# Seven-product feed-forward units: prefix sums in PSUM instead of partial sums in SBUF

## The chip, the cores and the metric

The kernel runs on one core of a Trainium2 chip. The metric is device time in microseconds (us) of one execution. The core has TensorE (matrix products into PSUM, the accumulator memory of eight banks), VectorE, ScalarE, GpSimd (POOL) and 16 DMA engines. All transfers are issued by SyncE (SP), which takes its instructions strictly in order: a transfer that has to wait for a buffer holds up every transfer behind it.

## The reference

Two layers, each of a gated long convolution (A) and a feed-forward block (B), over 2048 tokens of width 1024, all in 32-bit floats:

```python
x = A_q
x = x + _A_ref(_layernorm(x), A_k, A_v, A_shift_k, A_ssm_k, A_ssm_D)
x = x + _B_ref(_layernorm(x), B_w1, B_b1, B_w2, B_b2)
x = x + _A_ref(_layernorm(x), A_k, A_v, A_shift_k, A_ssm_k, A_ssm_D)
x = x + _B_ref(_layernorm(x), B_w1, B_b1, B_w2, B_b2)
...
def _B_ref(x, w1, b1, w2, b2):
    h = jnp.einsum("bsd,df->bsf", x, w1) + b1
    r = jnp.where(h > zero, h, zero)
    out = jnp.einsum("bsf,fd->bsd", r * r, w2) + b2
```

The hidden width of the feed-forward block is 3584. The change touches the second product (`w2`) alone.

## The kernel before

The tokens are cut into four blocks of 512 (`T`), and each block of each layer is a unit: eight units, in the order `ORDER`. A unit does the feed-forward block for its 512 tokens: the first product (`m1` steps), the squared ReLU, the second product (`m2` or `w2` steps), and the sum with the residual. The convolution for later blocks runs beside the first five units on VectorE, POOL, ScalarE and a little TensorE.

Every float32 product is made of three products of rounded parts (`mm3`, lines 335 to 338): a matrix is split into a high and a low part, and high x high, high x low and low x high are added in PSUM. A weight tile (128 x 512) is loaded into a ring of eight raw tiles (`wr`), cast by ScalarE into its high part (line 1013), and VectorE subtracts to make the low part (line 1021). High and low lie together in a `whl` tile, of which there are six. Some split weights are written back to DRAM (`wd_...`, lines 1025 to 1029) and later loaded as a pair of 512 KB, without a split (line 1011). Raw tiles are loaded 8 steps ahead, pairs asked for 4 steps ahead, once the `whl` slot is free.

The order is written out by hand: the list `steps` holds one step per weight tile, and each pass of the main loop issues one step to TensorE, with the loads and splits for later steps. Work that has to come later is put into `Later` queues with a number of ticks; one tick is one step. `lag.at(3, f)` issues `f` three steps on.

Units 5, 6 and 7 (`WINO`) make the second product with seven block products in place of eight (Winograd's form of Strassen's scheme). The 512 tokens are two halves, the hidden dimension goes in 14 pairs of tiles, the 1024 columns are two halves. Products 0 and 1 use plain parts of the activations and of `w2`, product 2 a sum of activations with plain `w2`, product 3 plain activations with a combined weight, and 4, 5 and 6 sums of activations with combined weights. Activations are combined on the fly (`relu_w`); combined weights are made once, in units 4 and 5 (`make_t`), and kept in DRAM (`td`). A unit has four chunks of 3, 3, 4 and 4 pairs (`WCH`): the first product for the chunk's tiles, and then the seven products in the order `WORD` (the last chunk: `WORD_END`), each over the chunk's pairs, for two tiles of 128 tokens, into two PSUM banks. Four banks (`p2`) serve products alternately.

After each product `evict_w` takes the two banks into SBUF: added by VectorE to a partial sum of that product, or, in chunk 0 for products 0, 4, 5 and 6, copied by ScalarE. Products 1, 2 and 3 and a tile `x` start from the residual plus the bias; products 0, 4, 5 and 6 have partial sums of their own (`fx`, `fg`, `acc`). In the last chunk the table `WEND` says after which product which partial sums are merged (`merge_w`, VectorE adds in SBUF) and when each quadrant (token half x column half) is stored. The residual is loaded at tick 11 (`load_wacc`), the bias `b2` at tick 34 into one of two `px` buffers, and POOL adds it at tick 38 (`add_b2w`). The same `px` buffers take the next unit's rows, loaded from step 28 of the unit on by `prep_a` for its statistics, and during the last 90 steps by `prep_w`, which normalises and transposes them.

In the last chunk of units 6 and 7, product 0 takes one stored pair and products 1, 4 and 5 take four each; the other weight tiles are raw. In unit 5, products 4 and 5 of the last chunk are split for the first time there and stored.

Of the kernel before, what the change touches and what calls it, by code (L numbers as in the profile page):

```python
# [10 lines left out]
F32 = mybir.dt.float32  # L11
# [8 lines left out]
P = 128  # L20
T = 512
NT = T // P
# [29 lines left out]
WINO = (5, 6, 7)  # L52
# [2 lines left out]
T_KEPT, T_RATE, T_FIRST, T_AT = 10, 0.6, 10, (0, 3, 1, 2)  # L55
WCH = (3, 3, 4, 4)
WHALF = T // 2
WORD, WORD_END = (0, 1, 3, 4, 5, 6, 2), (0, 3, 5, 6, 4, 2, 1)
WEND = {0: (), 3: (), 5: ((1, 1, 5, 0),), 6: ((1, 1, 6, 5), (2, 1, 3, 6), (2, 0, 3), (3, 1, 6, "x"), (3, 1, 1, 0)),
        4: ((1, 1, 6, 4), (1, 0, 6), (2, 1, 5, 4), (2, 1, 2, 5)), 2: ((1, 0, 2),), 1: ((1, 0, 1),)}  # L60
AHEAD_F = (6, 5)
KEEP_F = 3
KEEP_M = 4
# [177 lines left out]
def tile_h3_mlp(ctx: ExitStack, tc: tile.TileContext, q, kT, vT, shk, ssmT, ssmD, w1, b1, w2, b2,  # L241
                fwd_t, pro_t, inv_t, sgn_t, out):
    nc = tc.nc
    V, A, G, PE, SY = nc.vector, nc.scalar, nc.gpsimd, nc.tensor, nc.sync
# [65 lines left out]
    def ps2():  # L310
        return ps.tile([P, 512], F32, name="p2", bufs=4)
# [20 lines left out]
        for o in tiles:  # L332
            held[slot.pop(id(o))[0]] = False

    def mm3(o, lh, ll, rh, rl, start, stop):
        PE.matmul(o, lh, rh, start=start, stop=False)  # L336
        PE.matmul(o, lh, rl, start=False, stop=False)  # L337
        PE.matmul(o, ll, rh, start=False, stop=stop)  # L338

    def hold(n):  # L340
        got = take(n)
# [542 lines left out]
    def add_wino(u):  # L884
        p0 = 0
        for c, n in enumerate(WCH):
            pairs = range(p0, p0 + n)
            p0 += n
            for f in range(2 * pairs[0], 2 * pairs[-1] + 2):
                for kh in range(2):  # L890
                    add("m1", u, f // FC, f % FC, kh)
            for j in WORD_END if c == len(WCH) - 1 else WORD:
                for p in pairs:
                    f = 2 * p + (j > 0)
                    wsrc.append(("m2", f // FC, int(j == 2), f % FC) if j < 3 else ("t", p, (j - 4) % 4, 0))
# [593 lines left out]
    lag = slag  # L1489
# [94 lines left out]
            rp[p] = [(q["hi"], q["lo"]), (h(st["hi"], 0), h(lo, 0)), (st["zh"][:, 3], st["zl"][:, 3]),  # L1584
                     (h(st["hi"], 1), h(lo, 1)), *((st["zh"][:, i], st["zl"][:, i]) for i in range(3))]

    def load_wacc(wacc, b):
        for j, (t0, h) in {1: (0, 0), 2: (0, 1), 3: (2, 0), 0: (0, 0)}.items():
            a = ml.tile([P, 2, 512], F32, name="acc", bufs=NT)
            if j:  # L1590
                SY.dma_start(a, X1[b][:, t0:t0 + 2, h * 512:(h + 1) * 512])
            wacc[j] = [a[:, n] for n in range(2)]
        for j, mk in ((4, mkfx), (5, mkfx), (6, mkfg), ("x", mkfk)):
            wacc[j] = [mk([P, T]) for _ in range(2)]
        for n in range(2):
            SY.dma_start(wacc["x"][n], X1[b][:, 2 + n, 512:])

    def add_b2w(st, wacc):
        for j, h in ((1, 0), (2, 1), (3, 0), ("x", 1)):
            for a in wacc[j]:  # L1600
                G.tensor_add(a, a, st["t"][:, h * 512:(h + 1) * 512])  # L1601

    def evict_w(os, wacc, j, c):
        for n in range(2):
            if c == 0 and j in (0, 4, 5, 6):
                A.copy(wacc[j][n], os[n])
            else:
                V.tensor_add(wacc[j][n], os[n], wacc[j][n])

    def merge_w(wacc, dx):  # L1610
        d, x = dx
        for n in range(2):
            V.tensor_add(wacc[d][n], wacc[d][n], wacc[x][n])

    def store_w(wacc, l, b, j):
        t0, h = {1: (0, 0), 2: (0, 1), 3: (2, 0), 6: (2, 1)}[j]
        for n in range(2):
            dst = tokens(out, b, t0 + n) if l else X2[b][:, t0 + n]
            SY.dma_start(dst[:, h * 512:(h + 1) * 512], wacc[j][n])

    def evict(os, accs, dh):
        d = slice(dh * 512, (dh + 1) * 512)
# [145 lines left out]
    owed = town = 0.0  # L1768
    fowed = 0.0
    accs = []  # L1770
    pa = None
    nxt = None
    cur_u = -1
# [7 lines left out]
    for s, (k, u, c, a, i, tts, w) in enumerate(steps):  # L1781
        if s < 2 * AHEAD_0:
            continue
        l, b = ORDER[u]
        if u != cur_u:
            cur_u = u
            if u:
                xT = nxt
            bst = {}
            if u in WINO:  # L1790
                wacc, rp = {}, {}
                lag.at(11, load_wacc, wacc, b)
                lag.at(34, load_b2, bst)
                lag.at(38, add_b2w, bst, wacc)
            else:
                if not (u and direct[u - 1]):
                    accs = []
                    lag.at(5, load_acc, accs, b)
                lag.at(12, load_b2, bst)
                lag.at(16, add_b2, bst, accs)  # L1800
        soon.tick()
        phase[0] = "" if len(tts) == NT else "x" if k == "m1" else "b" if tts[0] else ""
        if phase[0] == "x":
# [7 lines left out]
        if k == "m1":  # L1811
            if len(tts) < NT:
                while not all(t in ready for t in tts):
                    lag.tick()
            xh, xl = xT
            t0, t1 = tts[0] * P, (tts[-1] + 1) * P
            if i == 0 and tts[0] == 0:
                bank = ps1 if len(tts) == NT else ps2 if a < 4 else lambda: spare.pop(0)
                rs[c, a] = {"o": bank(), "f": c * FC + a, "give": len(tts) < NT and a >= 4}
            o = rs[c, a]["o"]  # L1820
            for kk in range(4):
                t = slice(kk * P, (kk + 1) * P)
                mm3(o[:, t0:t1], wh[:, t], wl[:, t], xh[:, 4 * i + kk, t0:t1], xl[:, 4 * i + kk, t0:t1],
                    i == 0 and kk == 0, i == 1 and kk == 3)
            if i == 1 and u in WINO:
                for kk in range(4 if rs[c, a]["f"] % 2 else 2):
                    lag.at(1 + kk, relu_w, rs[c, a], kk, rp)
            elif i == 1 and tts[-1] == NT - 1:
                lag.at(1, relu2, rs[c, a], 0)
                lag.at(2, relu2, rs[c, a], 1)  # L1830
        elif k == "w2":
            done_at = sum(WCH[:c + 1])
            first = done_at - WCH[c]
            if i == first:
                os = [ps2() for _ in range(2)]
            while isinstance(rp.get(i, [None])[0], dict) and len(rp[i]) < 7:
                lag.tick()
            hi, lo = rp[i][a]
            for n in range(2):
                t = slice(n * P, (n + 1) * P)  # L1840
                mm3(os[n], hi[:, t], lo[:, t], wh, wl, i == first, i == done_at - 1)
            if i == done_at - 1:
                end = c == len(WCH) - 1
                lag.at(1, evict_w, os, wacc, a, c)
                if end:
                    last = u == NU - 1
                    for d, fn, *x in WEND[a]:
                        if fn:
                            lag.at(d if last else d + 3, merge_w, wacc, x)
                        else:  # L1850
                            lag.at(d + (0 if last and a == 1 else 3 if last else 6), store_w, wacc, l, b, x[0])
        else:
            turned = len(tts) < NT and tts[0] and a
            first, last = ((FC - KEEP_M) % FC, FC - KEEP_M - 1) if turned else (0, FC - 1)
            if i == first:
                os = {tt: ps2() for tt in tts}
            r = rs[c, i]
            for tt in tts:
                t = slice(tt * P, (tt + 1) * P)
                mm3(os[tt], r["hi"][:, t], r["lo"][:, t], wh, wl, i == first, i == last)  # L1860
            if i == last and direct[u] and c == NCH - 1:
                if a == tts[0] // 2:
                    cst = half(tts)
# [120 lines left out]
```

## Time and profile before

| | |
|---|---|
| median of 3 runs | 2709.59 us (2707.18 to 2711.41) |
| the profiled execution | 2710.68 us, its span 2708.9 us |
| TensorE busy | 2658.2 us (98%) |
| VectorE busy | 1988.0 us (73%) |
| ScalarE busy | 1124.1 us (41%) |
| POOL busy | 845.8 us (31%) |
| granted TensorE clock | 0.996 |
| DMA | 755.05 MB, mean 279 GB/s |

Busy time counts the time in which an engine has an instruction under way; matmuls overlap, so the distance of their starts tells more than their durations. In rows of instruction groups stand the line, the engine, the operation, output<-inputs, the count, busy time and mean duration in ns, then the idle time before and what ended it. In rows in order of time stand start, duration, engine and line, and in brackets the idle time before. In a list of waits stand who waited for whom, the total in us, how many times, and the longest. In a table by window stand the length, and for each engine the busy time and the number of instructions, and at the end the granted clock, the share of time that the DMA engines were busy, and GB/s. PEld is TensorE's weight load, SPq the queue of SP.

### The profile page before, as it was taken

The page shows a single profiled execution, that of the slowest core. Times are in us where ns is not written, and L with a number is a line of the kernel's source. Part 1 is how long each engine was busy: PE and PEld are TensorE (multiplying, and loading weights), DVE is VectorE, ACT ScalarE, POOL GpSimd, SP SyncE. Part 2 cuts the span into 40 slices and gives each one's busy share as a digit, 9 for nine tenths or more (in the row PEclk, how much of TensorE's full clock was granted, in tenths as well). Part 3 has the DMA queues.
Part 4 walks back from the last instruction along what each step waited for, and adds up shares of the span by engine and source line. Part 5 has one row for each costly group of instructions (what it writes and reads, how often), then busy time and mean ns, then how long its engine had stood idle before and what let it go on. Part 6 is the DMA issues. An engine that isn't in the chain of part 4 may idle for free.

```text
span 2708.9 us, 36533 instructions
## 1 busy us (share of the span) xinstructions
PE 2658.2 (98%) x12568; PEld 2227.5 (82%) x12568; DVE 1988.0 (73%) x3066; ACT 1124.1 (41%) x1936; POOL 845.8 (31%) x532
## 2 busy tenths in 40 slices
PE   7999999999999999999999999999999999999999
PEld 6888787888888888888888888888788788878887
DVE  7878888788987877779677765376787666664565
ACT  3454344433444233442234422244455444445443
POOL 2436565355632655236553454000000010001000
PEclk9999999999999999999999999999999999999999
DMA  8789898699999898788978887789888866676556
GB/s 250 262 305 314 290 311 279 234 308 372 333 305 321 300 342 285 266 334 289 354 263 276 298 304 248 237 295 310 294 286 300 278 231 212 231 270 210 179 167 206
DMA packets 377482, 755.05 MB, mean 279 GB/s; under 512 B 43840, under 2 KB 159184, under 8 KB 377296
## 3 DMA queue, kind: packets, MB, share of 16 engines
q1 hardware_dynamic: 377296, 752.72, 81.6%
q8 instruction: 99, 1.62, 0.2%
q14 instruction: 87, 0.71, 0.1%
HBM read 602.63 MB, written 149.95 MB: 278 GB/s over the span
## 4 chain that ended last, share of the span: by engine, by line
PE 82%; DMA 7%; DVE 6%; issue 2%; POOL 1%; ACT 1%; SPq 1%; DVEq 0%; ACTq 0%; POOLq 0%
PE p L336 25%; PE p L337 25%; PE p L338 25%; DMA wr<-w 2%; PE p L1097 2%; DVE whl L1021 1%; DMA whl<-wd_m 1%; PE pt L336 1%; PE pt L337 1%; PE pt L338 1%; DMA wd_m<-whl 1%; DMA whl<-wd_t 1%; DMA yt<-yd 0%; DMA wd_t<-whl 0%; DMA fx<-kT 0%
## 5 line engine op out<-in xcount | busy, mean ns | idle before, releaser
L526 POOL TENSOR_TENSOR cp<-cx,cg 128x384 f32<-128x384 f32 (+5 forms) x288 | 543.2, 1898 | 569.9 <-DVE sm L530 380.4
L336 PE MATMUL p<-xh,whl 128*128 128x512 f32 (+1 forms) x1840 | 707.6, 385 | 4.3 <-DMA whl<-wd_m 4.2
L338 PE MATMUL p<-xh,whl 128*128 128x512 f32 (+1 forms) x1840 | 703.8, 383 | 0.8 <-POOL whl L1021 0.8
L337 PE MATMUL p<-xl,whl 128*128 128x512 f32 (+1 forms) x1840 | 703.8, 383 | 0.1
L1013 ACT CAST whl<-wr 128x512 fp32r<-128x512 f32 x637 | 383.4, 619 | 437.0 <-PE p L338 308.5
L1021 DVE TENSOR_TENSOR whl<-wr,whl 128x512 fp32r<-128x512 f32 x622 | 500.9, 826 | 73.6 <-ACT whl L1013 69.2
L336 PE MATMUL p<-whl,rh 128*128 128x512 f32 x1372 | 541.2, 394 | 7.3 <-ACT whl L1013 3.7
L337 PE MATMUL p<-whl,rh 128*128 128x512 f32 x1372 | 536.6, 391 | 1.8 <-POOL whl L1021 0.8
L338 PE MATMUL p<-whl,rl 128*128 128x512 f32 x1372 | 536.0, 391 | 0.0
L336 PEld LDWEIGHTS p<-xh,whl 128*128 128x128 f32 x1840 | 347.0, 189 | 71.8 <-DMA whl<-wd_m 3.5
L338 PEld LDWEIGHTS p<-xh,whl 128*128 128x128 f32 x1840 | 346.6, 188 | 68.6 <-POOL whl L1021 1.0
L337 PEld LDWEIGHTS p<-xl,whl 128*128 128x128 f32 x1840 | 346.8, 188 | 65.6 <-DVE xl L1410 0.3
L336 PEld LDWEIGHTS p<-whl,rh 128*128 128x128 f32 x1372 | 258.7, 189 | 62.2 <-DMA whl<-wd_m 4.8
L337 PEld LDWEIGHTS p<-whl,rh 128*128 128x128 f32 x1372 | 258.7, 189 | 56.0 <-DVE whl L1021 3.4
L338 PEld LDWEIGHTS p<-whl,rl 128*128 128x128 f32 x1372 | 258.5, 188 | 54.3
L1504 DVE TENSOR_TENSOR rl<-wr,rh 128x512 fp32r<-128x512 f32 x140 | 145.8, 1042 | 178.3 <-ACT rh L1499 178.2
L1601 POOL TENSOR_TENSOR acc<-acc,px 128x512 f32<-128x512 f32 x18 | 23.2, 1325 | 766.6 <-DMA px<-b 766.6
L530 DVE TENSOR_REDUCE sm<-cp 128x128 f32<-128x384 f32 (+5 forms) x288 | 249.5, 874 | 10.9 <-POOL cp L526 10.9
L1496 ACT ACTIVATE wr<-p,b1t 128x512 f32<-128x512 f32 x138 | 95.2, 690 | 366.8 <-PE p L338 365.8
L1565 DVE TENSOR_TENSOR rl<-wr,rh 128x256 fp32r<-128x256 f32 x84 | 48.9, 582 | 211.2 <-ACT rh L1560 211.1
L1624 DVE TENSOR_TENSOR acc<-p,acc 128x512 f32<-128x512 f32 x152 | 99.8, 686 | 83.4 <-PE p L338 83.4
L1557 ACT ACTIVATE wr<-p,b1t 128x512 f32<-128x512 f32 x84 | 57.9, 689 | 191.0 <-PE p L338 190.9
(277 smaller groups left out, 3304.5 us busy)
## 6 DMA issues: line engine op xcount, KB each, us to landing
whl<-wd_m SPq DMA_DIRECT2D x379, 512.0 KB, 5.4
wr<-w SPq DMA_DIRECT2D x493, 256.0 KB, 5.4
wr<-td SPq DMA_DIRECT2D x152, 256.0 KB, 4.0
wd_m<-whl SPq DMA_DIRECT2D x70, 512.0 KB, 6.1
cx<-xd SPq DMA_DIRECT2D x48, 512.0 KB, 6.0
cg<-gd SPq DMA_DIRECT2D x48, 512.0 KB, 6.8
gd<-fg SPq DMA_DIRECT2D x72, 256.0 KB, 6.5
cx<-xd SPq DMA_DIRECT2D x48, 384.0 KB, 5.7
```

Source lines behind the costliest of these rows:

```text
L336: PE.matmul(o, lh, rh, start=start, stop=False)
L337: PE.matmul(o, lh, rl, start=False, stop=False)
L338: PE.matmul(o, ll, rh, start=False, stop=stop)
L526: G.tensor_mul(pr.rearrange("p c i -> p i c"), xt[:, 0:j + 1], gt[:, j::-1])
L530: V.tensor_reduce(sm[:, ty, jj], st["pr"], axis=AX.X, op=OP.add)
L1013: A.copy(t[:, 0], raws[n]["t"])
L1021: ENG[e[n % len(e)]].tensor_sub(t[:, 1], raws[n]["t"], t[:, 0].bitcast(F32))
L1097: PE.matmul(o, lh, r, start=start, stop=stop)
L1496: A.activation(r, st["o"], AF.Relu, bias=b1t[:, st["f"]:st["f"] + 1])
L1504: V.tensor_sub(st["lo"], st["r"]["t"], st["hi"].bitcast(F32))
L1557: A.activation(r, st["o"], AF.Relu, bias=b1t[:, st["f"]:st["f"] + 1])
L1624: V.tensor_add(accs[tt][:, d], o, accs[tt][:, d])
```

## The change

The seven products are taken in the order 0, 1, 5, 4, 6, 2, 3 in every chunk, the last included. Two pairs of banks stay open over a chunk. In pair "b" product 5 is added onto product 0, then 6, then 3, without clearing; in pair "f" product 1 stands alone, then 4 begins anew and 2 is added onto it. After each product the bank's content at that moment, a prefix of the sum, is added by VectorE straight to the one quadrant that needs it (`WSUM`); no product has a partial sum of its own, and nothing is merged. All evictions are VectorE adds. The accumulators are the whole rows that the other units use (`load_acc` at tick 5, `add_b2` with 1024 columns per add on POOL); the bias is loaded at tick 7 and added at tick 11. A quadrant is stored three ticks after its last product (one in the last unit): quadrants are complete after products 1, 2, 6 and 3.

```diff
-WORD, WORD_END = (0, 1, 3, 4, 5, 6, 2), (0, 3, 5, 6, 4, 2, 1)
-WEND = {0: (), 3: (), 5: ((1, 1, 5, 0),), 6: ((1, 1, 6, 5), (2, 1, 3, 6), (2, 0, 3), (3, 1, 6, "x"), (3, 1, 1, 0)),
-        4: ((1, 1, 6, 4), (1, 0, 6), (2, 1, 5, 4), (2, 1, 2, 5)), 2: ((1, 0, 2),), 1: ((1, 0, 1),)}
+WORD = (0, 1, 5, 4, 6, 2, 3)
+WBANK = {0: "b", 5: "b", 6: "b", 3: "b", 1: "f", 4: "f", 2: "f"}
+WOPEN = (0, 1, 4)
+WSUM = {0: (0, 0), 1: (0, 0), 5: (0, 1), 2: (0, 1), 6: (2, 1), 4: (2, 1), 3: (2, 0)}
+WDONE = (1, 2, 6, 3)
...
-            for j in WORD_END if c == len(WCH) - 1 else WORD:
+            for j in WORD:
...
-    def load_wacc(wacc, b):
...
-    def add_b2w(st, wacc):
...
-    def evict_w(os, wacc, j, c):
-        for n in range(2):
-            if c == 0 and j in (0, 4, 5, 6):
-                A.copy(wacc[j][n], os[n])
-            else:
-                V.tensor_add(wacc[j][n], os[n], wacc[j][n])
-
-    def merge_w(wacc, dx):
-        d, x = dx
+    def evict_w(os, accs, j):
+        t0, h = WSUM[j]
         for n in range(2):
-            V.tensor_add(wacc[d][n], wacc[d][n], wacc[x][n])
+            a = accs[t0 + n][:, h * 512:(h + 1) * 512]
+            V.tensor_add(a, os[n], a)
...
-            if u in WINO:
-                wacc, rp = {}, {}
-                lag.at(11, load_wacc, wacc, b)
-                lag.at(34, load_b2, bst)
-                lag.at(38, add_b2w, bst, wacc)
-            else:
-                if not (u and direct[u - 1]):
-                    accs = []
-                    lag.at(5, load_acc, accs, b)
-                lag.at(12, load_b2, bst)
-                lag.at(16, add_b2, bst, accs)
+            rp = {}
+            if not (u and direct[u - 1]):
+                accs = []
+                lag.at(5, load_acc, accs, b)
+            b2_at = (7, 11) if u in WINO else (12, 16)
+            lag.at(b2_at[0], load_b2, bst)
+            lag.at(b2_at[1], add_b2, bst, accs)
...
-            if i == first:
-                os = [ps2() for _ in range(2)]
+            if i == first and WBANK[a] not in open_w:
+                open_w[WBANK[a]] = [ps2() for _ in range(2)]
+            os = open_w[WBANK[a]]
...
-                mm3(os[n], hi[:, t], lo[:, t], wh, wl, i == first, i == done_at - 1)
+                mm3(os[n], hi[:, t], lo[:, t], wh, wl, i == first and a in WOPEN, i == done_at - 1, a not in WOPEN)
             if i == done_at - 1:
-                end = c == len(WCH) - 1
-                lag.at(1, evict_w, os, wacc, a, c)
...
+                lag.at(1, evict_w, os, accs, a)
+                if a == WORD[-1]:
+                    open_w.clear()
+                if c == len(WCH) - 1 and a in WDONE:
                     last = u == NU - 1
...
+                    lag.at(1 if last else 3, store_w, accs, l, b, a)
```

More of the change, by code (lines that the diff above doesn't have):

```diff
@@ L333, in give, with mm3 @@
             held[slot.pop(id(o))[0]] = False
[L335 to L338, printed above, removed]
+    def mm3(o, lh, ll, rh, rl, start, stop, skip=False):
+        PE.matmul(o, lh, rh, start=start, stop=False, skip_group_check=skip)
+        PE.matmul(o, lh, rl, start=False, stop=False, skip_group_check=skip)
+        PE.matmul(o, ll, rh, start=False, stop=stop, skip_group_check=skip)
     def hold(n):
@@ L1585, in relu_w, with store_w @@
                      (h(st["hi"], 1), h(lo, 1)), *((st["zh"][:, i], st["zl"][:, i]) for i in range(3))]
-    def load_wacc(wacc, b):
[L1588 to L1594, printed above, removed]
-        for n in range(2):
-            SY.dma_start(wacc["x"][n], X1[b][:, 2 + n, 512:])
-    def add_b2w(st, wacc):
-        for j, h in ((1, 0), (2, 1), (3, 0), ("x", 1)):
-            for a in wacc[j]:
-                G.tensor_add(a, a, st["t"][:, h * 512:(h + 1) * 512])
-    def evict_w(os, wacc, j, c):
-        for n in range(2):
-            if c == 0 and j in (0, 4, 5, 6):
-                A.copy(wacc[j][n], os[n])
-            else:
-                V.tensor_add(wacc[j][n], os[n], wacc[j][n])
-    def merge_w(wacc, dx):
-        d, x = dx
[L1612 to L1616, printed above, removed]
+    def evict_w(os, accs, j):
+        t0, h = WSUM[j]
+        for n in range(2):
+            a = accs[t0 + n][:, h * 512:(h + 1) * 512]
+            V.tensor_add(a, os[n], a)
+    def store_w(accs, l, b, j):
+        t0, h = WSUM[j]
         for n in range(2):
             dst = tokens(out, b, t0 + n) if l else X2[b][:, t0 + n]
-            SY.dma_start(dst[:, h * 512:(h + 1) * 512], wacc[j][n])
+            d = slice(h * 512, (h + 1) * 512)
+            SY.dma_start(dst[:, d], accs[t0 + n][:, d])
     def evict(os, accs, dh):
@@ L1770, in tile_h3_mlp @@
     accs = []
+    open_w = {}
     pa = None
@@ L1840, in tile_h3_mlp @@
                 t = slice(n * P, (n + 1) * P)
-                mm3(os[n], hi[:, t], lo[:, t], wh, wl, i == first, i == done_at - 1)
+                mm3(os[n], hi[:, t], lo[:, t], wh, wl, i == first and a in WOPEN, i == done_at - 1, a not in WOPEN)
             if i == done_at - 1:
-                end = c == len(WCH) - 1
-                lag.at(1, evict_w, os, wacc, a, c)
-                if end:
+                lag.at(1, evict_w, os, accs, a)
+                if a == WORD[-1]:
+                    open_w.clear()
+                if c == len(WCH) - 1 and a in WDONE:
                     last = u == NU - 1
[L1847 to L1851, printed above, removed]
+                    lag.at(1 if last else 3, store_w, accs, l, b, a)
         else:
```

## The prediction

> **What bounds the kernel now.** I read the page's busy times first, then the matmul starts in order of time, the busy time by stage, and the waits of TensorE in the last three units.
>
> ```profile
> span 2708.9 us, 36533 instructions
> PE 2658.2 (98%) x12568; PEld 2227.5 (82%) x12568; DVE 1988.0 (73%) x3066; ACT 1124.1 (41%) x1936; POOL 845.8 (31%) x532
> ```
>
> TensorE is busy for 98% of the span, VectorE for 73%. The change keeps every matmul, so VectorE's work is worth something only where TensorE stands still for it. Next, the first and the last of 197 consecutive matmuls, and then stages of units 5 to 7 (first number after the window: its length).
>
> ```profile
> 1839.67 0.39 PE L336 MATMUL p<-xh,whl 128*128 128x512 f32 x1
> ...
> 1884.09 0.39 PE L337 MATMUL p<-whl,cx 128*128 128x512 f32 x1
> ```
>
> ```profile
> 1887.30:1924.60 37.30, 34.49 (x145) 28.07 (x144) 21.73 (x45) 13.36 (x22) 10.66 (x8) 0.95 0.88 315
> 2185.70:2218.50 32.80, 32.80 (x145) 26.94 (x144) 17.02 (x36) 13.36 (x22) 10.28 (x8) 1.00 0.73 265
> 2157.10:2185.50 28.40, 28.40 (x127) 23.49 (x127) 18.44 (x32) 17.26 (x30) 0.00 (x0) 1.00 0.60 192
> 1924.60:1953.50 28.90, 28.85 (x127) 23.58 (x126) 25.21 (x47) 13.07 (x21) 0.00 (x0) 1.00 0.79 243
> 2079.00:2124.40 45.40, 42.79 (x201) 34.45 (x200) 38.85 (x65) 24.77 (x42) 0.00 (x0) 1.00 0.83 300
> 2372.60:2417.10 44.50, 42.59 (x201) 34.40 (x200) 35.43 (x58) 20.75 (x34) 0.00 (x0) 1.00 0.78 266
> 2665.10:2704.90 39.80, 39.45 (x169) 30.96 (x167) 28.51 (x47) 10.05 (x16) 0.00 (x0) 1.00 0.74 251
> ```
>
> 196 intervals in 44.42 us: a matmul every 0.2266 us. A step of the second product (six matmuls on one weight tile) is 1.36 us, a step of the first (twelve) 2.72 us. Against that floor:
> - First product of chunk 1, 144 matmuls, floor 32.6: 37.3 in unit 5, 32.8 in unit 6. Unit 5 loses 4.7.
> - Second product of chunks 0 and 1, 126 matmuls, floor 28.6: chunk 0 of unit 6 has no excess (28.4, a window cut short), chunk 1 of unit 5 has 0.3.
> - Second product of the last chunk, 168 matmuls, floor 38.1. In units 5 and 6 the next unit's transposes stand in between, four groups like the one below, at 0.8 each: floor 41.3. Excess 4.1, 3.2 and 1.7 for units 5, 6 and 7, together 9.0.
>
> ```profile
> 2378.12 0.93 PE L854 MATMUL p<-ident,px 128*128 128x128 f32 x7
> 2378.80 0.47 PE L336 MATMUL p<-whl,rh 128*128 128x512 f32 x1
> ```
>
> Some 15 us of standing still is all that this change can win here, 0.55% of the time.
>
> ```profile
> PE p L336 <- DMA whl<-wd_m: 7.2, 6, 2.8
> ...
> PEld p L336 <- DMA whl<-wd_m: 8.3, 6, 3.2
> PEld p L336 <- DMA whl<-wd_t: 2.6, 6, 0.7
> PEld p L337 <- DVE whl L1021: 2.3, 5, 0.5
> PEld p L336 <- DVE acc L1608: 2.2, 2, 1.5
> ```
>
> So in units 5 to 7 TensorE and its weight loads wait mostly for stored weight pairs that come back by DMA, and for VectorE only 4.5 us (splits 2.3, evictions 2.2). What matters is when pairs are asked for and what stands ahead of them, not the merges.
>
> **The change part by part.**
>
> *Evictions and merges.*
>
> ```profile
> L1608 DVE TENSOR_TENSOR acc<-p,acc 128x512 f32<-128x512 f32 x90 | 59.1, 685 | 26.6 <-PE p L338 26.6
> L1606 ACT COPY fx<-p 128x512 f32<-128x512 f32 x12 | 7.0, 587 | 7.8 <-PE p L338 7.2
> L1613 DVE TENSOR_TENSOR fg<-fg,fx x12: 682/686/696, 2107.5 to 2696.8; 128x512 f32<-128x512 f32 x12
> ```
>
> By the code a unit has 56 evictions (four chunks, seven products, two banks), 8 of them copies on ScalarE, and 16 merges. After: 56 evictions, all on VectorE, no merge. VectorE loses 16 x 0.69 us in the last chunk and gains 8 x 0.69 in chunk 0; none of it is on TensorE's path by itself. In chunk 0 the ScalarE copies freed banks without VectorE; now chunk 0 is like chunk 1, which has that arrangement and loses 0.3. Three chunks: +1.0 (from 0 to 2). Banks: products still alternate between two pairs, and each has one product's time (4.1 us or more) to be read before the pair is written again, as before. Cost 0; the cover is an eviction that keeps up, and the 2.2 above is what it costs when it doesn't.
>
> *The bias load, from tick 34 to tick 7.* This is what unit 5 lost 4.7 to:
>
> ```profile
> SPq L726 <- POOL fk L1601: 8.1, 1, 8.1
> ...
> 1890.38 0.32 SPq L726 DMA_DIRECT2D px<-x  x1
> ...
> 1902.40 0.32 SPq L726 DMA_DIRECT2D px<-x  x1
> 1902.82 1.36 SPq L1011 DMA_DIRECT2D whl<-wd_m  x1
> ...
> 1899.38 2.99 POOL L1601 TENSOR_TENSOR fk<-fk,px 128x512 f32<-128x512 f32 x2
> ...
> 1909.27 0.50 PE L336 MATMUL p<-xh,whl 128*128 128x512 f32 x1 [2.81 <-DMA whl<-wd_m]
> ...
> 1911.11 0.63 PE L336 MATMUL p<-xh,whl 128*128 128x512 f32 x1
> 1911.53 0.63 PE L337 MATMUL p<-xl,whl 128*128 128x512 f32 x1
> ```
>
> The bias shares two `px` buffers with the next unit's rows. The fourth row load waits 8.1 us at the head of SP until POOL has added the bias (1902.37), the weight pair behind it is issued at 1902.82, and TensorE goes on at 1909.27 after 2.81 us of idling. After that matmuls start 0.42 apart for a while, and the granted clock of the whole window is 0.95: 5% of 37.3 is 1.9. Together they make the 4.7. With the bias added in chunk 0 the `px` buffers are free when the rows come; late next is the statistics of the row before, which costs unit 6 at most 0.2 here. I take -4.4 (from -4.7 to 0).
>
> The Trainium skill, "TensorE: Matmul & The Clock Gate", section "What's actually happening", has the clock at half after one idle window of about 3.4 us. Here 2.8 us of idling were enough, so a stall near 3 us is priced with the slow matmuls behind it.
>
> *Accumulator loads, from tick 11 to tick 5, one tile per 128 tokens.* Same bytes (2 MB), now two steps after the previous unit's last store, so that SP can wait for that store, and with two pair loads of the unit's first stage behind it.
>
> ```profile
> acc<-x SPq DMA_DIRECT2D x25, 512.0 KB, 7.3
> ...
> whl<-wd_m SPq DMA_DIRECT2D x379, 512.0 KB, 5.4
> ```
>
> A pair is asked for when the weight six places ahead has been used, five steps or 13.6 us before its use in this stage. A wait of one landing (7.3) and its own 5.4 make 12.7: just hidden. I take +0.5 for unit 5, where DMA is fullest (0 to 2).
>
> *The order of the last chunk's products.* It was 0,3,5,6,4,2,1 and becomes 0,1,5,4,6,2,3. In units 6 and 7 products 1, 5 and 4 take stored pairs (512 KB a step), 0 takes one, and 3, 6, 2 single tiles (256 KB and a split). Three bursts of four pairs, two of them apart, become one burst of twelve. In unit 5 products 5 and 4 are stored for the first time (256 KB read and 512 KB written a step), now back to back.
>
> ```profile
> 2372.60:2378.00 5.40, 5.40 (x25) 4.42 (x24) 3.16 (x7) 5.17 (x8) 0.00 (x0) 1.00 0.06 8
> 2416.10:2421.60 5.50, 4.47 (x20) 3.74 (x21) 1.99 (x4) 0.89 (x2) 0.00 (x0) 1.00 1.04 409
> ...
> DMA to landing us min/median/max: 3.3/6.2/8.0
> ...
> 2673.49 7.14 DMA whl<-wd_t
> 2680.66 0.50 PE p L336
> ...
> SPq L1619 <- DVE acc L1613: 4.5, 2, 4.3
> ```
>
> DMA moves 409 GB/s when full, so 512 KB takes 1.28 us, less than a step of 1.36; with a single tile 1.92. The chunk opens with DMA idle (8 GB/s), room for the first pairs, which aren't held by the ring of raw tiles. Landing is 3.3 at the least, and five steps are 6.8 us; the 7.14 above came with a 256 KB load behind each pair and cost little. In a burst of twelve the single tiles for product 6 are asked for in the last four steps: 4 x (1.92 - 1.36) = 2.2 us of backlog, two row loads in unit 6 another 2.6, so 3.3 + 2.2 + 2.6 = 8.1 against 6.8. I take 1.5 for unit 6. Unit 7 has no rows, but its first quadrant is stored one step after product 1, in front of the ninth pair (in the old order SP stood 4.3 at such a store behind a merge). SP waits some 1.5 for the evictions and issues for 0.9; pairs that could go at once go 2.4 late, with 512 KB more ahead of them (1.3): 3.3 + 2.2 + 2.4 + 1.3 = 9.2 against 6.8, 2.4. For unit 5, eight steps of 1.92 build 4.5 us, which eight raw tiles ahead (10.9 us) mostly cover: 1.5. Against that, the old stalls at the end of the chunk go, since it now ends with single tiles asked for long before. 5.4 in place of 9.0: -3.6 (from -9.0, no stall, to +8.9, the second rival).
>
> The Trainium skill, "DMA: Bandwidth & Descriptors", section "Bandwidth", gives 358 GB/s from HBM for a core whose neighbour streams too. By it a pair would take 1.46 us, and the two bursts 2 x 12 x 0.1 = 2.4 us more. The 409 above disagrees; no such limit binds this core.
>
> *Stores* by quadrant at tick 3 (tick 1 in the last unit): same bytes, same last pair of evictions and stores behind the last matmul. Cost 0, beside what is in the terms above.
>
> **The sum.** +1.0 - 4.4 + 0.5 - 3.6 = -6.5. The profiled execution took 2710.68 (span 2708.9), so 2704.2; it lies 1.09 above the median shown (2709.59), against which I forecast 2703.1. From no change a measurement here tells about 0.2%, 5.4 us.
>
> **The rivals.**
> 1. *The burst eats what the end of the chunk gives.* Pairs land near 8 us rather than under 7, and the three last chunks stay at 9.0. Then -4.4 + 1.0 + 0.5 = -2.9: 2706.7. For it: the 7.14 landing with four pairs. Against: DMA idle as the chunk opens.
> 2. *Slower: DMA becomes the bound of the last chunks.* If single tiles run beside all twelve pairs, each step takes 1.92: 12 x 0.56 = 6.7 in each of units 6 and 7, 4.5 in unit 5, 17.9 in place of 9.0. Sum -2.9 + 8.9 = +6.0: 2715.6. It decides once pairs land later than 6.8 us through the whole burst. For it: the 409 GB/s with TensorE idle at the end of the old last chunk. Against: raw tiles run only eight steps ahead.
> 3. *The bias was not what held SP*, or another wait takes its place there: -6.5 + 4.4 = -2.1, 2707.5. Against it: 1902.37 and 1902.40.
>
> **How the numbers follow.** My forecast 0.5 (2698 to 2706 by itself), the first rival 0.22, the second 0.2, the third 0.08. The forecast's case is faster by over 5.4 us nearly always; rivals 1 and 3 lie within; the second is slower. Low: -4.7 - 9.0 is 2695.9; high: the second rival, 2715. Faster 0.5, same 0.3, slower 0.2.
>
> **What would show it.** Right: unit 5's chunk 1 at 32.8, no wait of SP's row load for POOL there, the three last chunks at some 42.8, 42.8 and 40.5, chunk 0 at 28.9, and no VectorE wait at the end of the chunks. Wrong: waits for `whl<-wd_t` of several us in units 6 and 7, slow matmuls behind them, or VectorE adds that wait for a store of the other half of the same accumulator.

## The result, and the profile after

| | before | after |
|---|---|---|
| median of 6 runs each | 2708.39 us (2706.27 to 2711.41) | 2717.95 us (2714.83 to 2720.7) |
| the profiled execution, its span | 2710.68, 2708.9 us | 2718.27, 2716.5 us |

The changed kernel is slower: ratio 1.0035, 95% interval 1.0022 to 1.0048. The forecast was 2703.1 us, its range ended at 2715. The medians differ by 9.6 us, the spans by 7.6; what follows works with the two profiled executions.

The first rows of the page of after:

```profile
span 2716.5 us, 36547 instructions
PE 2660.4 (98%) x12568; PEld 2227.2 (82%) x12568; DVE 1984.6 (73%) x3042; ACT 1114.5 (41%) x1912; POOL 848.3 (31%) x520
```

VectorE has the 24 instructions fewer that the change promised (16 merges less 8 evictions, three times), and TensorE does the same 12568 matmuls. Nothing here says where 7.6 us went; the stages do. In this table a stage lasts from its first matmul to the first of the next stage (the last one to one matmul interval behind its last matmul), by the matmul starts of each trace (numbers in us):

| stage | before | after | difference | predicted |
|---|---|---|---|---|
| chunk 0, second product, units 5, 6, 7 | 28.56, 28.56, 28.56 | 34.29, 30.23, 30.36 | +9.2 | +1.0 |
| chunk 1, first product, unit 5 | 37.35 | 32.64 | -4.7 | -4.4 |
| last chunk, second product, units 5, 6, 7 | 45.40, 44.56, 39.75 | 45.65, 44.82, 43.22 | +4.0 | -3.6 |
| all else in units 5 to 7 | | | -0.4 | +0.5 |
| all before unit 5 | 1826.07 | 1825.61 | -0.5 | 0 |

Chunk 0 of the three units, the first product of unit 5's chunk 1 and the last chunks of units 5 and 7 by window (columns: length, then busy time and number of instructions of PE, PEld, DVE, ACT and POOL, the granted clock, the DMA share, GB/s), of after:

```profile
1858.30:1892.50 34.20, 31.01 (x127) 24.54 (x126) 32.91 (x59) 17.18 (x28) 1.18 (x1) 0.95 0.74 244
2157.90:2188.10 30.20, 29.13 (x127) 23.49 (x126) 24.79 (x42) 14.97 (x26) 0.00 (x0) 1.00 0.65 200
2452.30:2482.60 30.30, 29.14 (x127) 23.46 (x126) 24.18 (x41) 15.14 (x26) 0.00 (x0) 1.00 0.60 183
1892.50:1925.20 32.70, 32.70 (x146) 27.05 (x146) 20.07 (x47) 13.46 (x22) 0.00 (x0) 1.00 1.00 368
2079.60:2125.30 45.70, 42.98 (x202) 34.56 (x201) 29.39 (x48) 25.51 (x42) 0.00 (x0) 1.00 0.98 355
2669.30:2712.50 43.20, 39.22 (x169) 31.04 (x167) 19.37 (x31) 10.45 (x16) 0.00 (x0) 1.00 0.70 247
```

In unit 5 VectorE is busy for 32.91 of the 34.20 us of chunk 0, the time in which its instructions are held up included, and the granted clock has gone to 0.95. Chunk 1's first product (fourth row) now runs without a gap, with the DMA engines busy all the time (1.00): a full DMA is no loss by itself. Of the waits of TensorE in unit 5's chunk 0:

```profile
PEld p L339 <- DVE whl L1023: 4.5, 3, 2.5
PE p L339 <- DVE whl L1023: 3.2, 3, 2.1
```

TensorE waits for VectorE's split of a weight tile. What VectorE does just ahead of it, in order of time (start, duration), and POOL beside it, of after:

```profile
1849.22 10.26 POOL L1725 TENSOR_TENSOR acc<-acc,px 128x1024 f32<-128x1024 f32 x4 [156.97 <-DMA px<-b]
...
1849.61 2.57 DVE L1567 TENSOR_TENSOR rl<-wr,rh 128x512 fp32r<-128x512 f32 x1 [4.44 <-ACT rh L1562]
1852.10 2.61 DVE L1572 TENSOR_TENSOR yl<-wr 128x256 f32<-128x256 f32 x1
1854.75 2.50 DVE L1573 TENSOR_TENSOR yl<-yl,wr 128x256 f32<-128x256 f32 x1
1857.18 2.58 DVE L1574 TENSOR_TENSOR yl<-wr 128x256 f32<-128x256 f32 x1
1859.68 0.41 DVE L1575 TENSOR_TENSOR yl<-wr,yl 128x256 f32<-128x256 f32 x1
```

And the same instructions of before, where POOL has nothing at that time:

```profile
1850.07 0.69 DVE L1565 TENSOR_TENSOR rl<-wr,rh 128x512 fp32r<-128x512 f32 x1 [4.44 <-ACT rh L1560]
1850.68 0.42 DVE L1570 TENSOR_TENSOR yl<-wr 128x256 f32<-128x256 f32 x1
1851.13 0.42 DVE L1571 TENSOR_TENSOR yl<-yl,wr 128x256 f32<-128x256 f32 x1
```

Adds of 256 columns take 2.5 us in place of 0.42, as long as POOL's bias adds (10.26 us for four) are under way, and 0.41 as soon as they are over at 1859.48. All held instructions have two inputs in SBUF. Four of them lose 8.3 us of VectorE's time at the opening of the second product, where the sums and splits of the first pairs are due. The split of the stage's first weight tile starts only at 1860.02, so TensorE has done the first matmul with its high part and goes on with the low part at 1860.75:

```profile
1858.25 0.39 PE L338 MATMUL p<-whl,rh 128*128 128x512 f32 x1
1860.75 0.50 PE L339 MATMUL p<-whl,rh 128*128 128x512 f32 x1 [2.11 <-DVE whl L1023]
...
1862.36 0.63 PE L339 MATMUL p<-whl,rh 128*128 128x512 f32 x1
1862.79 0.63 PE L340 MATMUL p<-whl,rl 128*128 128x512 f32 x1
```

A stall of 2.11 us, and from 1862.4 on matmuls 0.43 apart in place of 0.23 for some 3 us. The waits' 3.2 us and 5% of 34.2 us (1.7) make 4.9 of the 5.7 by which this stage grew. In units 6 and 7 the clock stays at 1.00; there POOL is done some 3 us before the stage opens (in unit 6 at 2154.75, against 2157.89), and TensorE still waits 1.1 and 1.2 us for VectorE's late splits.

The Trainium skill, "SBUF — State Buffer", section "Who interferes with whom", says that VectorE and GpSimd share a pair of ports into SBUF, that the pair is an exclusive lock, and that a VectorE instruction with two SBUF inputs contends there with a GpSimd instruction that reads SBUF. The trace agrees: 0.42 became 2.5 us, about one POOL add (10.26 / 4 = 2.57).

The last chunk of unit 7. SP's queue of after in order of time, and then the matmuls that waited for a transfer:

```profile
2673.56 4.40 SPq L1013 DMA_DIRECT2D whl<-wd_t  x4
2680.48 1.01 SPq L1600 DMA_DIRECT2D out<-acc  x2
2681.90 0.33 SPq L1013 DMA_DIRECT2D whl<-wd_t  x1
```

```profile
2687.56 0.47 PE L338 MATMUL p<-whl,cx 128*128 128x512 f32 x1 [1.78 <-DMA whl<-wd_t]
2690.16 0.51 PE L338 MATMUL p<-whl,cg 128*128 128x512 f32 x1 [0.98 <-DMA whl<-wd_t]
...
2694.71 0.50 PE L338 MATMUL p<-whl,cg 128*128 128x512 f32 x1 [0.94 <-DMA whl<-wd_t]
```

SP issues nothing from 2677.96 to 2680.48: it stands at the store of the first quadrant until that quadrant's evictions are done, and the next pair is asked for at 2681.90. Pairs then come late four times, 4.0 us in all.

### The profile page after: what moved, and what is told of

Read it like the earlier page. It is cut to its first block, busy times and chain, and to the rows that moved or that the text cites. A ratio compares the mean times of both kernels' runs of the same rounds, so it can differ in the third digit from the quotient of the medians.

```text
span 2716.5 us, 36547 instructions
## 1 busy us (share of the span) xinstructions
PE 2660.4 (98%) x12568; PEld 2227.2 (82%) x12568; DVE 1984.6 (73%) x3042; ACT 1114.5 (41%) x1912; POOL 848.3 (31%) x520
## 4 chain that ended last, share of the span: by engine, by line
PE 80%; DVE 7%; DMA 7%; issue 2%; POOL 2%; ACT 1%; SPq 1%; DVEq 0%; POOLq 0%; ACTq 0%
PE p L339 24%; PE p L340 24%; PE p L338 24%; PE p L1099 2%; DVE whl L1023 1%; DMA wr<-w 1%; DMA cg<-gd 1%; DMA whl<-wd_t 1%; PE pt L338 1%; PE pt L340 1%; PE pt L339 1%; POOL cp L528 1%; DVE sm L532 1%; DMA whl<-wd_m 1%; DMA yt<-yd 0%
## 5 line engine op out<-in xcount | busy, mean ns | idle before, releaser
L1023 DVE TENSOR_TENSOR whl<-wr,whl 128x512 fp32r<-128x512 f32 x622 | 499.9, 826 | 71.2 <-ACT whl L1015 65.7
L1725 POOL TENSOR_TENSOR acc<-acc,px 128x1024 f32<-128x1024 f32 x32 | 84.8, 2681 | 738.2 <-DMA wr<-w 568.5
L1506 DVE TENSOR_TENSOR rl<-wr,rh 128x512 fp32r<-128x512 f32 x140 | 138.5, 990 | 183.7 <-ACT rh L1501 183.5
L1498 ACT ACTIVATE wr<-p,b1t 128x512 f32<-128x512 f32 x138 | 95.3, 690 | 367.2 <-PE p L340 366.4
L1593 DVE TENSOR_TENSOR acc<-p,acc 128x512 f32<-128x512 f32 x168 | 111.7, 687 | 67.7 <-PE p L340 67.6
L1605 DVE TENSOR_TENSOR acc<-p,acc 128x512 f32<-128x512 f32 x152 | 99.8, 686 | 82.2 <-PE p L340 82.2
```

The costliest lines, as they stand in the source:

```text
L1023: ENG[e[n % len(e)]].tensor_sub(t[:, 1], raws[n]["t"], t[:, 0].bitcast(F32))
L1498: A.activation(r, st["o"], AF.Relu, bias=b1t[:, st["f"]:st["f"] + 1])
L1506: V.tensor_sub(st["lo"], st["r"]["t"], st["hi"].bitcast(F32))
L1593: V.tensor_add(a, os[n], a)
L1605: V.tensor_add(accs[tt][:, d], o, accs[tt][:, d])
L1725: G.tensor_add(a, a, st["t"])
```

## The experiments

Two questions: what makes chunk 0 longer (POOL's bias adds, or the eight evictions that came from ScalarE to VectorE), and what makes the last chunks longer (the store ahead of the pairs in SP's queue, the twelve stored pairs in a row, or the prefix sums themselves). Not all runs were on one chip, so each has runs of the kernel before on the same chip beside it; stage lengths are those of the profiled execution. The part ahead of unit 5, which no edit touches, lasts from 1823.7 to 1828.1 us in these executions, so a span alone can mislead by some 4 us. A first product that nothing holds up comes back at 32.64 us each time, and chunk 0 without POOL's adds at 28.9 to 29.1. The last chunks are not so steady: in the six executions whose edits don't touch them (the changed kernel, the four edits of its bias add, the ScalarE copies) they take 44.75 to 46.05, 44.13 to 44.85 and 42.26 to 43.22 us in units 5, 6 and 7. A difference there counts only where it is clear of that spread; by it the last chunks of units 5 and 6 (45.40 and 44.56 before) did not change, and unit 7's (39.75) did.

**The bias late again.** Everything else of the change stays.

```diff
-            b2_at = (7, 11) if u in WINO else (12, 16)
+            b2_at = (34, 38) if u in WINO else (12, 16)
```

> The changed kernel with one part undone: the bias is loaded at tick 34 and added by POOL at tick 38 again (units 5 to 7). Theory A (POOL's adds at tick 11 hold up VectorE's SBUF work just ahead of chunk 0's second product): that stage, 34.2, 30.2 and 30.3 us in units 5, 6 and 7 of the changed kernel, falls to 28.9 in each, and unit 5's first product of chunk 1 goes back from 32.7 to some 37; about 2714 us. Theory B (VectorE has too much since it took over ScalarE's evictions in chunk 0): the three stages stay at 34.2, 30.2, 30.3 and unit 5 loses the 4.7 on top; about 2722 us.

Measured: 2712.41 us against 2707.83 (ratio 1.0016, 1.0005 to 1.0026). Chunk 0 takes 28.91, 28.91 and 28.90 us: 8.2 of the 9.2 us are gone. The first product of chunk 1 goes from 32.64 back to 34.47 in unit 5 and 33.49 in unit 6. So the early bias is what lengthens chunk 0, and the late bias lengthens chunk 1: SP's row load waits 7.3 us for POOL again. But of unit 5's 4.7 us only 1.8 come back, where I had expected some 37 us: TensorE idles 1.31 us here in place of 2.81, and no slow matmuls follow (granted clock 1.00).

**No bias add on POOL in units 5 to 7.**

```diff
-            lag.at(b2_at[1], add_b2, bst, accs)
+            if u not in WINO:
+                lag.at(b2_at[1], add_b2, bst, accs)
```

> The changed kernel without POOL's bias add in units 5 to 7 (the load stays; the output lacks b2 there). Theory A: the second product of chunk 0 takes 28.9 us or less in all three units; about 2709.5 us. Theory B: 34.2, 30.2 and 30.3 as before, 2718 us.

The output lacks that bias in these units. Measured: one run of 2709.18 us. Its chunk 0 of unit 5:

```profile
1857.80:1886.70 28.90, 28.85 (x127) 23.58 (x126) 25.97 (x48) 13.53 (x22) 0.00 (x0) 1.00 0.78 260
```

28.9 in all three units, and the clock back at 1.00. The load of the bias was still there, so it is the adds.

**ScalarE copies in chunk 0 again**, with POOL's adds left at tick 11. The copies overwrite the accumulator, so a part of the sum is left out.

```diff
-            V.tensor_add(a, os[n], a)
+            if c == 0 and j in (0, 4, 5, 6):
+                A.copy(a, os[n])
+            else:
+                V.tensor_add(a, os[n], a)
```

> The changed kernel with chunk 0's evictions of products 0, 4, 5 and 6 as ScalarE copies (they overwrite the accumulator, so a part of the sum is left out). Theory A: VectorE still starts the stage late, so chunk 0 keeps most of its excess: 33 or more in unit 5, 29.3 or more in units 6 and 7; 2714 to 2717 us. Theory B: 28.6 in all three, 2709 us.

Measured: one run of 2717.17 us; chunk 0 takes 33.45, 29.41 and 29.40 us. The copies give back 0.8 and 1.0 us in units 6 and 7 while POOL holds VectorE up, and 0.35 where it doesn't (28.56 of before against 28.9 of the two runs above). Unit 5's 0.8 is no fair comparison, as the granted clock there is 1.00 in this run and 0.95 in after. VectorE is busy for only 28.87 us of that stage, and the stage is still long: VectorE's work comes late, there is not too much of it. The evictions are the small part, 1.0 us over three units, which is what the prediction had for them.

**POOL's adds in halves**, at the same tick: eight adds of 512 columns in place of four of 1024.

```diff
+    def add_b2h(st, accs):
+        for a in accs:
+            for h in range(2):
+                d = slice(h * 512, (h + 1) * 512)
+                G.tensor_add(a[:, d], a[:, d], st["t"][:, d])
...
-            lag.at(b2_at[1], add_b2, bst, accs)
+            lag.at(b2_at[1], add_b2h if u in WINO else add_b2, bst, accs)
```

> The changed kernel with the bias added by POOL in 512-column pieces (eight of about 1.3 us in place of four of 2.6) at the same tick 11. If a VectorE instruction with two SBUF inputs waits for the POOL instruction under way and then goes, it now waits half as long each time, and the chain of five ahead of chunk 0's second product in unit 5 is through some 4 us sooner: that stage falls from 34.2 to some 30, units 6 and 7 from 30.2 to 29 to 30; held-up instructions show 1.0 to 1.5 us, not 2.5. If VectorE is merely slowed in proportion to POOL's busy time, nothing changes: 34.2, 30.2, 30.3.

Measured: one run of 2719.1 us; chunk 0 takes 33.52, 30.39 and 30.21 us, no better. Chunk 0 of unit 5, then VectorE and POOL of this run:

```profile
1860.70:1894.30 33.60, 29.76 (x128) 23.30 (x128) 33.02 (x57) 15.56 (x26) 2.76 (x2) 1.00 0.74 245
...
1851.33 12.14 POOL L1727 TENSOR_TENSOR acc<-acc,px 128x512 f32<-128x512 f32 x8 [156.56 <-DMA px<-b]
...
1853.09 1.51 DVE L1572 TENSOR_TENSOR yl<-wr 128x256 f32<-128x256 f32 x1
1854.63 1.39 DVE L1573 TENSOR_TENSOR yl<-yl,wr 128x256 f32<-128x256 f32 x1
...
1858.82 3.48 DVE L1023 TENSOR_TENSOR whl<-wr,whl 128x512 fp32r<-128x512 f32 x2
```

A held instruction now takes 1.5 us, as long as one half add (12.14 / 8), which fits two engines that take turns, one instruction each. But POOL's work lasts 12.14 us in place of 10.26, and more of VectorE's instructions fall into it, the splits (L1023) too. My expectation of a shorter chunk was wrong. And the clock is at 1.00 here, after a stall of 2.30 us: the stage is nearly as long as in after without the slow matmuls, as TensorE stands idle for 3.8 us of it in place of 3.2.

**The bias in tiles of its own.** The bias is loaded at tick 7 into two `fx` tiles that the change left idle, and added by POOL at tick 38, from the end of chunk 0 into chunk 1's first product. So nothing of SP waits for POOL, and POOL stays out of the opening of chunk 0.

```diff
+    def load_b2w(st):
+        st["t"] = [mkfx([P, T]) for _ in range(2)]
+        for h in range(2):
+            SY.dma_start(st["t"][h], bass.AP(tensor=b2.tensor, offset=b2.offset + h * 512, ap=[[0, P], [1, 512]]))
...
+            if u in WINO:
+                lag.at(7, load_b2w, bst)
+                lag.at(38, add_b2w, bst, accs)
```

> The changed kernel with the bias loaded at tick 7 into two idle fx tiles and added by POOL at tick 38, 512 columns at a time, so that neither the px buffers nor chunk 0 see it. Theory A: chunk 0's second product 28.9 in all three units, and unit 5's first product of chunk 1 stays at 32.7: 8.3 us less than the changed kernel, about 2709.5 us. Theory B: 34.2, 30.2, 30.3 stay, 2718 us.

Measured: 2709.34 us against 2707.83 (ratio 1.0006, 0.9995 to 1.0016). Chunk 0 takes 29.06, 28.90 and 28.89, and chunk 1's first product stays at 32.64 in all units. POOL still holds VectorE up, now where there is slack; its rows in order of time show which instructions:

```profile
1882.71 9.68 POOL L1731 TENSOR_TENSOR acc<-acc,fx 128x512 f32<-128x512 f32 x7 [14.61 <-DVE acc L1593]
...
1886.26 1.23 DVE L1593 TENSOR_TENSOR acc<-p,acc 128x512 f32<-128x512 f32 x2
1887.41 1.14 DVE L1537 TENSOR_TENSOR yt<-yt 128x256 f32<-128x256 f32 x1
1888.59 1.40 DVE L1538 TENSOR_TENSOR yt<-yt 128x256 f32<-128x256 f32 x1
```

The two evictions (L1593), with one input in PSUM, take 1.23 us beside a POOL add, no longer than elsewhere (two took 1.28 in unit 7 of after, where POOL is idle); the subtractions with both inputs in SBUF take 1.1 to 1.4 in place of 0.42. This closes the first question: 8.0 of the 9.2 us in chunk 0 are POOL's, and nothing had to be paid for them elsewhere. What is left over before is the last chunks, 46.04, 44.85 and 42.34 us here.

**The first quadrant stored late**, on top of the bias in its own tiles: nine ticks after product 1, behind most of the pair loads.

```diff
-                    lag.at(1 if last else 3, store_w, accs, l, b, a)
+                    lag.at(9 if a == 1 else 1 if last else 3, store_w, accs, l, b, a)
```

> e4_bias_fx (bias kept out of the way) with one more edit: the quadrant that is complete after product 1 is stored nine ticks after it, behind all pair loads of the last chunk, not one or three. The last chunk's second product takes 46.0, 44.9 and 42.3 us in units 5, 6 and 7 of e4_bias_fx. Theory S (SP stands at that store and the pairs behind it go late): unit 7 falls to some 40, unit 6 to some 43.5, unit 5 stays; about 2705.5 us. Theory D (twelve pairs in a row ask for more than DMA delivers): all three stay within 0.5; 2709 us.

Measured: 2703.74 us against 2708.58 (ratio 0.9989, 0.998 to 0.9998). The last chunks take 44.61, 42.89 and 40.61 us: -1.4, -2.0 and -1.7. SP's queue in unit 7, to be held against that of after above:

```profile
2663.14 5.76 SPq L1013 DMA_DIRECT2D whl<-wd_t  x5
2668.96 0.42 SPq L1002 DMA_DIRECT2D wr<-td  x1
2669.94 0.32 SPq L1013 DMA_DIRECT2D whl<-wd_t  x1
...
2678.39 2.39 SPq L1600 DMA_DIRECT2D out<-acc  x2
```

The hole of 2.5 us after the fourth pair is gone: in unit 7 SP stood at the store (S in the expectations). In unit 6 the gain is clear of the spread too, but SP did not stand there; its queue in unit 6 of after:

```profile
2387.17 0.49 SPq L1002 DMA_DIRECT2D wr<-td  x1
2387.76 0.97 SPq L1600 DMA_DIRECT2D out<-acc  x2
2390.16 0.33 SPq L1013 DMA_DIRECT2D whl<-wd_t  x1
```

The store goes out 0.1 us after the load ahead of it. It takes 0.97 us to issue, and the next pair follows 1.43 us later, a wait that the profile puts down to a row load, not to the store. With the store moved away, the two pairs behind it are asked for 1.9 and 2.2 us sooner in the stage than with the bias in its own tiles alone; why by so much stays open. The 44.61 of unit 5, which has no pairs behind that store, is just below the spread of the last chunks, so no gain is shown there.

**Another order in the last chunk**, on top of the bias in its own tiles: 0, 4, 5, 2, 6, 1, 3, so that eight pairs and four pairs have single tiles between them.

```diff
-WORD = (0, 1, 5, 4, 6, 2, 3)
+WORD, WORD_END = (0, 1, 5, 4, 6, 2, 3), (0, 4, 5, 2, 6, 1, 3)
...
-            for j in WORD:
+            for j in WORD_END if c == len(WCH) - 1 else WORD:
```

> e4_bias_fx with the last chunk's products in the order 0, 4, 5, 2, 6, 1, 3: eight pairs in a row and four later, in place of twelve. Theory D: units 6 and 7 fall to about 43 and 40.5, unit 5 stays near 46; about 2705.5 us. Theory S: the store that lies ahead of pairs is now that behind product 2, with four pairs behind it in place of eight: unit 7 about 41.3, unit 6 about 44.5; 2708 us.

Measured: 2709.68 us against 2708.58 (ratio 1.0005, 0.9996 to 1.0014). The last chunks take 46.33, 43.62 and 42.69 us: -1.2 in unit 6 (0.5 below the spread), +0.3 in the two others. Neither theory fits both units 6 and 7; in unit 7 twelve against eight in a row is not what counts.

**No stored pairs for products 4 and 5**, on top of the bias in its own tiles: their weights of the last chunk are taken as single tiles and split each time.

```diff
-T_KEPT, T_RATE, T_FIRST, T_AT = 10, 0.6, 10, (0, 3, 1, 2)
+T_KEPT, T_RATE, T_FIRST, T_AT = 14, 0.6, 10, (0, 3, 1, 2)
```

> e4_bias_fx without stored pairs for products 4 and 5: no store of pairs in unit 5, and in units 6 and 7 their weights are loaded raw (256 KB) and split by ScalarE and VectorE (eight splits more per unit). Theory D: the last chunks fall to about 42.5, 43 and 39.5 us; about 2704 us. Theory S: the store now stands ahead of raw tiles that are asked for eight steps ahead, so unit 7 falls to some 40 too, but units 5 and 6 keep 45.5 and 44.5; 2706.5 us. If VectorE becomes the bound instead, units 6 and 7 take longer than 44.9 and 42.3.

Measured: 2700.43 us against 2708.58 (ratio 0.9973, 0.9964 to 0.9982), faster than both kernels. The last chunks:

```profile
2073.10:2116.80 43.70, 42.35 (x202) 34.70 (x201) 29.53 (x48) 25.82 (x42) 0.00 (x0) 1.00 0.81 274
2365.00:2406.70 41.70, 41.70 (x201) 34.76 (x200) 29.38 (x48) 25.85 (x42) 0.00 (x0) 1.00 0.82 285
2654.90:2693.60 38.70, 38.38 (x169) 31.29 (x168) 24.00 (x39) 15.25 (x24) 0.00 (x0) 1.00 0.65 221
```

Unit 6 has no gap left, unit 7 0.3. DMA is busy for 0.81 of unit 5's last chunk in place of 0.98. The price is VectorE's: 24.00 us of splits and evictions in unit 7 in place of 19.37, and it hides.

**Both: no pairs for 4 and 5, and the late store.**

```diff
-T_KEPT, T_RATE, T_FIRST, T_AT = 10, 0.6, 10, (0, 3, 1, 2)
+T_KEPT, T_RATE, T_FIRST, T_AT = 14, 0.6, 10, (0, 3, 1, 2)
...
-                    lag.at(1 if last else 3, store_w, accs, l, b, a)
+                    lag.at(9 if a == 1 else 1 if last else 3, store_w, accs, l, b, a)
```

> e7_no_kept with the late store of e5_store_late as well. Theory D alone: as e7_no_kept, about 2704 us. Theory S alone: as e5_store_late. Both: the last chunks near 42, 42.5 and 39, about 2703 us, less than either kernel of the case.

Measured: 2700.84 us against 2708.58 (ratio 0.9975, 0.9966 to 0.9983); last chunks 43.56, 41.92 and 39.01. Without the pairs the early store costs nothing (0.1 to 0.4 us either way): raw tiles are asked for eight steps ahead. With the pairs it costs 2.0 and 1.7 us in units 6 and 7, so there a short lead and something in front cost together. With the store out of the way the pairs still cost 1.0, 1.0 and 1.6 us (44.61, 42.89 and 40.61 against the lengths here), about the spread of a last chunk.

**The kernel before without those pairs.** Merges, order and bias of before; only the pairs are gone.

```diff
-T_KEPT, T_RATE, T_FIRST, T_AT = 10, 0.6, 10, (0, 3, 1, 2)
+T_KEPT, T_RATE, T_FIRST, T_AT = 14, 0.6, 10, (0, 3, 1, 2)
```

> The kernel before without stored pairs for products 4 and 5 (as e7_no_kept, but with partial sums, merges and the old order). It tells what the prefix sums themselves are worth at the end of a unit. If the merges cost nothing, the last chunks come out as in e7_no_kept (43.7, 41.8 and 38.7 us); if VectorE's 16 adds in the last chunk cost time once it has eight splits more, they are longer, by up to 16 x 0.6 = 9.6 us in all VectorE can't hide. Unit 5 keeps its 37.3 in chunk 1. I expect 44.5, 43 and 39.5, 2704 us.

Measured: 2707.35 us against 2708.53 (ratio 0.9998, 0.9989 to 1.0008). The last chunks take 42.86, 42.90 and 39.63 us, 4.3 less than before, though the time of whole runs does not show it. Against the changed kernel without the pairs (43.68, 41.75, 38.65) the prefix sums gain 1.15 in unit 6 and 1.0 in unit 7 and lose 0.8 in unit 5: 1.3 us in three units, and chunk 0 takes 1.2 of it back (28.9 against 28.56). These are one execution each, and differences of that size lie near the spread. So the thing that the change is named for is worth about nothing here. The 3.7 us by which that version is ahead in these stages are mostly unit 5's chunk 1 (36.09 against 32.64), that is, the bias. The medians of the two lie 6.9 us apart, on two chips; in the profiled executions 3.6 us of the difference stand ahead of unit 5, which neither edit touches.

## Why the prediction was wrong

It gave 2703.1 and the other sign. By its own steps:

1. **Evictions and merges: +1.0. Right.** Chunk 0 without POOL's adds takes 28.9 in place of 28.56 in each unit. That VectorE's merges are not on TensorE's path was right too, as far as the runs without the stored pairs show (1.3 us in sum over three units, order and merges together).
2. **The bias load to tick 7: -4.4. Right for what it looked at, and the step that failed most.** Unit 5's chunk 1 went from 37.35 to 32.64, -4.7, and SP no longer stands there for POOL. Some of that hangs on the slow matmuls of that execution of before: with the same late bias and the clock at 1.00, the kernel before without the pairs took 36.09, 3.5 more than 32.64. But the step moved a load and the adds behind it, and I costed only the load: POOL's four adds went along, from chunk 1's first product to the opening of chunk 0, and there they hold VectorE's adds of two SBUF tiles for 2.5 us each. That costs +8.2 over three units (9.2 less the 1.0 of step 1). I had looked for what waits for POOL, and found SP; I did not ask what POOL holds up just by running.
3. **Accumulator loads at tick 5: +0.5, from 0 to 2. Nothing seen:** the first stage of each unit is at 32.64.
4. **The order of the last chunk: -3.6. Wrong in sign, +4.0.** The excess over the floor is 4.4, 3.6 and 5.1 us in units 5, 6 and 7, 13.1 in place of 9.1, where I had 1.5, 1.5 and 2.4. The gains that I had for units 5 and 6 did not come (+0.3 each, within the spread), and the loss is unit 7's (+3.5). For unit 7 the mechanism was the one I gave (the first quadrant's store in front of the ninth pair, SP standing there 2.5 us), but I had less than half its size (2.4 against 5.1), and late storing, tried with the bias in its own tiles, takes back 1.7 us. For unit 6 I had the store down as free at tick 3, and it takes 2.0. And the pairs, which I had as just in time, are worth 2.4, 3.1 and 3.7 us in units 5, 6 and 7, as taking them out shows; with the store late 1.0, 1.0 and 1.6 of it remain.
5. **Stores: 0.** Wrong by the 2.0 us of unit 6; unit 7's 1.7 were in step 4.

The sum with the measured terms: +9.2 - 4.7 + 0 + 4.0 = +8.5, less 0.4 in other stages and 0.5 ahead of unit 5: 7.6, the difference of the spans.

The second rival, slower by DMA at 2715.6, came closest in number and was not what happened. It had 8.9 us for the last chunks; 4.0 came from there, and 8.2 from a place that no rival had. DMA was near its limit in unit 5's last chunk alone (0.98 busy), and 0.87 and 0.70 in units 6 and 7. The first rival, that the burst takes the gain back, is the nearest for the last chunks. The third is excluded: the bias was what held SP.

The chances had 0.2 for slower. What was missing is in the list of what is moved: POOL's adds stand in the diff one line below the load. And the trace of before shows the effect in chunk 1's first product, beside the same POOL adds (1891.71 to 1902.37), where slack hid it:

```profile
1894.73 1.05 DVE L1565 TENSOR_TENSOR rl<-wr,rh 128x256 fp32r<-128x256 f32 x1 [3.39 <-ACT rh L1560]
...
1901.15 1.50 DVE L1570 TENSOR_TENSOR yl<-wr 128x256 f32<-128x256 f32 x1
1902.69 0.43 DVE L1571 TENSOR_TENSOR yl<-yl,wr 128x256 f32<-128x256 f32 x1
```

The add of 256 columns takes 1.50 us with POOL busy and its neighbour 0.43 once POOL is done. Whoever moves POOL's adds can read there what they will do to VectorE, and that at the new place four such adds stand ahead of the first splits.

Two more readings of the prediction need a word. It prices a stall near 3 us with slow matmuls behind it. They followed the stall of 2.81 us in before and that of 2.11 in after, but not those of 2.12 (the other order), 2.13 (ScalarE copies), 2.30 (adds in halves) and 2.58 us (before without the pairs), where the granted clock stayed at 1.00; so the price is not a fixed one. And it sets its 409 GB/s against a figure for a core whose neighbour streams too. Only one core runs here, so the two don't contradict each other, and the sum didn't use that figure.

Open: why the store ahead of the pairs costs 2.0 us in unit 6, where SP hardly stands at it; what the rest of the pairs' cost is; and what decides whether the clock falls after a stall of some 2 to 3 us.

## What to carry to other kernels

When a step is moved, list every instruction that it issues, and for each ask not only who waits for it but whom it holds up by running where it now runs: a GpSimd add over SBUF made the VectorE adds of two SBUF tiles beside it about as long as itself here, so it belongs where VectorE has slack, not at the opening of a stage that lives on VectorE's first results. In an in-order transfer queue a store should come behind loads with a short lead, above all one that must wait for its data; loads asked for eight steps ahead did not notice it, pairs asked for four steps ahead did. And a new buffer for a small operand (the bias) solved both ends of a move that each cost more than the change could win.

## What the runs showed of the hardware

- GpSimd and VectorE: VectorE adds of 256 columns with two SBUF inputs took 2.5 us beside GpSimd adds of 1024 columns and 1.5 beside adds of 512, in place of 0.42; adds with one input in PSUM were not held (1.23 for two, as without GpSimd). Cutting GpSimd's adds in half made its work 12.14 us long in place of 10.26 and won nothing.
- The clock: after a stall of 2.11 us (after) and one of 2.81 us (before) TensorE ran matmuls 0.42 to 0.43 us apart for some 3 us, and the granted clock of the window was 0.95. After stalls of 2.12, 2.13, 2.30 and 2.58 us in four other runs it did not. The length of the stall alone does not decide it.
